# A fused spectral mixer and Mish MLP on one core: w1's first pieces in four transfers, idle matmuls on a built-in constant, the last tile in three column pieces, a new task order

## The chip, the cores and the metric

The kernel runs on one core of one Trainium2 chip. The metric is device time in microseconds, the median over several executions. A profile is one further execution, taken by the hardware profiler. Engines in the profile: PE is TensorE's matmul, PEld its weight load, DVE is VectorE, ACT is ScalarE, POOL is GpSimd, SP is SyncE; ACTq and SPq are the DMA issues of those two.

## The reference, cut to what matters

```python
# x: (1, 2048, 512) bf16
g = sigmoid((x * gate_w).sum(-1, keepdims=True))
a = irfft2(rfft2(x) * (w_r + 1j * w_i), s=(2048, 512))        # spectral branch
h = x @ w1 + b1                                               # w1: 512 x 1792
b = (h * tanh(softplus(h))) @ w2                              # Mish; w2: 1792 x 512
out = g * a + (1 - g) * b
```

## The kernel before, in words

The 2048 rows are 16 tiles of 128 (`NT`), the 1792 hidden columns 14 pieces (`NFT`), the dense branch runs in 4 chunks of 4 tiles (`NCH`). Both branches share TensorE.

Head. SyncE issues the loads of x and most others in a fixed order; ScalarE issues the first pieces of w1 (`ld_w1(0, 4, ...)`, one transfer of 256 rows for each half h of d) and one later piece. GpSimd loads b1 (`braw`). The load of ScalarE's function table (`table`) is a task on ScalarE like any other. Until x is there TensorE runs matmuls whose result nobody reads (`warm0` and on, L425); `NWARM` of them have 256 columns, `NFILL` have 128. They read a tile of zeros that a memset on DVE (L417) makes. Then `tr*` (L476) transpose x, `tr_small` (L484) transposes b1, and `evx*` copy the transposes into `xT`, on DVE or ScalarE.

Dense branch. `mm1_c_ft` (L773) multiplies xT by a piece of w1; `mish_c_ft` (L788) applies Mish on ScalarE into `act`; `mm2_t_0` and `mm2_t_1` (L803) sum the 14 pieces for tile t. In chunk 0 the pieces ft 0 to 3 are cut in four: `mm1a` is tiles 0 and 1, `mm1b` tiles 2 and 3, and the digit behind is the half h of d. For most tiles `bev_t` scales the result out of PSUM (L755 on ScalarE, L756 on DVE) and `sum_t` adds the spectral part; for the last two tiles `fin` (L815) does both in one DVE step. The last tile is computed and stored in two halves of 256 columns.

Spectral branch. `a10`, `a11` (L512) and `s1` (L538) transform forward and go through scratch in DRAM (`r1w`, `r1r`); `s2` (L635) is the second stage; DVE multiplies by the filter (`wm`), GpSimd combines (`wz`), `s2i` (L695) goes back; a second trip through scratch (`r2w`, `r2r`); `s1i` (L723) and `a1i` (L734) finish, with `e5`, `gc`, `sa` and `sb` between and behind.

Order. Each operation is a task with an engine, dependencies and, where it writes PSUM, a bank. The order of every engine, the engine of tasks that can run on either of two, and the banks are not found at build time: they are read from the string `ORDER`, two digits in base 62 for a task, a letter for its engine where there is a choice, a digit for its bank. Each engine runs its tasks strictly in that order. A wait is placed ahead of a task where one of its inputs, or the bank it takes, comes from another engine. `DENSE` and `DENSE2` list the banks that a planner may give to dense products; the digit in `ORDER` decides.

Of the kernel before, what the change touches and what calls it, by code (L numbers as in the profile page):

```python
# [7 lines left out]
BF = mybir.dt.bfloat16  # L8
# [5 lines left out]
NT = 16  # L14
# [151 lines left out]
class _Graph:  # L166
# [89 lines left out]
DIGITS = "0123456789ABCDEFGHIJKLMNOPQRSTUVWXYZabcdefghijklmnopqrstuvwxyz"  # L256
ENGINE = {"p": "pe", "a": "act", "v": "dve", "g": "pool", "s": "sp"}
ORDER = (
    "020L0M0T0500O060N070P03080R090A0Q000B040C010S0D0E0F0U0G0V0H2y0w30W0y70I0J0xv0X0K6k50Y6z11046p00Z11a0a0zv1220b6"
    "u313v1G7701H711Jv6l0c6m721Iv6v736w6x6n6y1K40d7420e1M6o1L10f1461Nv750g1630h15v7670i1Ov1U40j1V27717v1850k1Pv0l1e"  # L260
    "v1W7810m1fv0n7A31Xv0o790p1Yv1A67B0q1C10r1Bv1Za1r70s1Dv1g41i0t19v7C20u2i7E37D20v7G62j7F6q21v1q47H1h26r1s1kv6s7I"
    "16t2k1la7K31jv7J2l7M47L1uv2322m7N2252D67a0241vv1tv1E126v7b25v27v7c37e07d1Fv2C72n7f1Q27g12E2Mv7i01Rv7h331a47j2G"
    "v7k11S1ba2Fv7m02Nv1T7l2Hv1m22o1c7n2O62Y71nv1d7o12Q2a2Z02p7q57p1o2cv1p2P11w32Rv7r7s62Sv1xa7u72dv2bv7t1y2822q7v2"
    "I41z29v7w12Ta2Ja2U62r7x2A7y32Vv2B2e17z2K8002s2fa2L8E62t2W818G72u2X8F2v2g8I58H2h2w8K18J2x8L2z8M2388O0398N3A8Q78"
    "P3B8S68R30318U1328T0v8V347358W4368Y2378X8a08Z3C38b3D63E8c53Mv8e18d3F3Qv3G7O08f3Pv7P3Lv3Sg3H23Y67Qa3I3Ng3Z43a7R"
    "23hv3Rg3b7S3c3mv3Og3d17U07Ta3e3J3iv3K3T7V3lv3jg3U43kg7Wa7X13Wa3Vv3ng3X3u63v23og7Y3w44v3f43v3g8s07Za3p3x48v3q44"
    "5g8t8u13sa3rv46g8w08v47v4G43t8x3y4H68y14Tv4Ag3z28208z4Pv49g834J404I4Qv414K424B9014Uv4Sg4L4922914M84v4N4C44Wg93"
    "8514Da4Ev4O4Vg4F864X4Rg94087a4Y4958814Za4av4b898B08Aa8C4c4d4e8g18Da4f963982979A0999C59B4g34o49D9E04hv4pa4i54w3"
    "9F5444q64xv4j8h55a4l4r4k4t5C04ng5K48ia4s4y55625Dv4mg5La5S38j15Tv4z4vg57514ug505E7595a453g5F5i3585U65ba8k5jv52g"
    "5V5G5Bg5X5H8m05Ag8la5W9av9bv5k59ev5M29c5l8n9dv5N5Ig9f5P5Jg5O8p18oa5Zg5m5n5Rg5c25q49gv5y55d6635Qg5ra5zv9G667a5f"  # L270
    "5pg6055e9H9I75Yg615s39hv8q9J635hg9i5t629jv5v5gg6E68ra5u6M49K764g6Nv6Fa9kv5xg9l6816U3699L5og6Vv6A5wg6B6c365g9Ma"
    "6W56G49N09nv6da9pv6H9mv6X6I6Dg9O9o6Z6Y6Cg6J6ag6O76e39Pa9Q29qv6f6bv9r6P6Lg6g6R9R6Kg6Q6h6Tg9U59sv9S6ig6jv9T9X16S"
    "g9V9W9tv9u9Y9Z"
)
NBF = 14
GD_N = 8
# [5 lines left out]
A1B = (3, 4, 5, 6, 7)  # L282
SPEC = (3, 4, 5, 6, 7)
DENSE = {0: (0, 1, 2, 3), 1: (0, 1), 2: (0, 1), 3: (0, 1)}
DENSE2 = {0: (0, 1), 1: (0, 1), 2: (0, 1), 3: (0, 1)}
NWARM = 12
NFILL = 4
PR = dict(tr=99.0, sp=95.0, mm1=88.0, mish=97.0, mm2=70.0, fin=98.0, gate=96.9, sum=98.5)


def _build(nc, A_x, A_w_r, A_w_i, B_x, B_w1, B_b1, B_w2, gate_w, out):
# [6 lines left out]
    G = _Graph()  # L298
    es = ExitStack()
    with es:  # L300
# [86 lines left out]
        def mm(n):  # L387
            return n / 2400.0 + 0.0025
# [10 lines left out]
        def pe(name, dur, fn, **kw):  # L399
            return G.add(name, "pe", dur, fn, lat=0.17, **kw)  # L400
# [6 lines left out]
        def tt(name, o, i0, i1, op, n, rate=1.0, engs=("dve",), lock=True, **kw):  # L407
# [9 lines left out]
        G.add("wz", "dve", 0.3, lambda e: e.memset(act[:, 2, 0, :], 0.0), writes=["warm"])  # L417
        G.add("ebz", "pool", 0.2, lambda e: e.memset(b1f[:, 0:1], 0.0), writes=["b1z"])
        t_tab = G.add("table", "act", 1.3, lambda e: e.activation(b1f[:, 1:2], b1f[:, 0:1], AF.Mish), reads=["b1z"], writes=["b1t"], prio=0.0)

        pw = _Ps([6])
        tw = []
        for i in range(NWARM + NFILL):
            n = 256 if i < NWARM else 128
            tw.append(pe(f"warm{i}", mm(n), lambda e, n=n: e.matmul(ps[:, pw.bank, 0:n], act[:, 2, 0, 0:128], act[:, 2, 0, 0:n], start=True, stop=True),  # L425
                         reads=["warm"], alloc=pw if i == 0 else None, frees=[pw], prio=0.0, deps=tw[-1:]))
# [5 lines left out]
        def ld_w1(lo, hi, queues):  # L432
            cols = slice(128 * lo, 128 * hi)
            for h in range(2):
                dma(f"ld_w1_{lo}_{h}", w1_sb[:, 2 * h:2 * h + 2, cols], w1v[:, h, :, cols],
                    writes=[("w1", f, h) for f in range(lo, hi)], nbytes=65536 * (hi - lo), bw=340e3, nd=256, queue=queues[h])

# [326 lines left out]
        for c in range(NCH):  # L764
            hb = c % 3
            G.cur_prio = PR["mm1"] - c
            for ft in range(NFT):
                pd = _Ps(DENSE[c])

                def f_mm1(e, c=c, ft=ft, pd=pd, cols=(0, 512), ks=range(4)):  # L770
                    ins = None
                    for i in ks:
                        ins = e.matmul(ps[:, pd.bank, cols[0]:cols[1]], w1_sb[:, i, 128 * ft:128 * (ft + 1)], xT[:, i, 512 * c + cols[0]:512 * c + cols[1]],  # L773
                                       start=(i == 0), stop=(i == 3))
                    return ins

                pr_m = PR["mm1"] - c - 0.06 * ft
                if c == 0 and ft < 4:
                    for part in range(2):
                        for h in range(2):  # L780
                            pe(f"mm1{'ab'[part]}{h}_{ft}", 2 * mm(256), lambda e, f=f_mm1, part=part, h=h: f(e, cols=(256 * part, 256 * part + 256), ks=(2 * h, 2 * h + 1)),
                               reads=[("xT", 2 * part + i, h) for i in range(2)] + [("w1", ft, h)], writes=[("pm", c, ft), ("pmx", ft, part, h)],
                               alloc=pd if part == h == 0 else None, prio=PR["mm1"] + 1.0 - 0.3 * part - 0.06 * h - 0.01 * ft)
                else:
                    pe(f"mm1_{c}_{ft}", 4 * mm(512), f_mm1, reads=[("xT", 4 * c + i, q) for i in range(4) for q in range(2)] + [("w1", ft, 0), ("w1", ft, 1)],
                       writes=[("pm", c, ft)], alloc=pd, deps=mm2s.get(c - 3, ()), prio=pr_m)
                G.add(f"mish_{c}_{ft}", "act", act_dur(512, True),
                      lambda e, ft=ft, pd=pd, hb=hb: e.activation(act[:, hb, ft, :], ps[:, pd.bank, :], AF.Mish, bias=b1f[:, ft:ft + 1]),  # L788
                      reads=[("pm", c, ft), "b1f"], writes=[("act", hb, ft)] + (["warm"] if hb == 2 and ft == 0 else []), frees=[pd], prio=PR["mish"])
            G.cur_prio = PR["mm2"] - c  # L790
            for tl in range(4):
                t = 4 * c + tl

                for part in range(2):
                    if part == 0 or t == NT - 1:
                        pd = _Ps(DENSE2[c])
                    cs_ = slice(256 * part, 256 * part + 256) if t == NT - 1 else slice(0, 512)
                    fts = range(NFT) if t == NT - 1 else range(7 * part, 7 * part + 7)

                    def f_mm2(e, tl=tl, hb=hb, pd=pd, cs_=cs_, fts=fts):  # L800
                        ins = None
                        for ft in fts:
                            ins = e.matmul(ps[:, pd.bank, cs_], act[:, hb, ft, 128 * tl:128 * (tl + 1)], w2_sb[:, ft, cs_],  # L803
                                           start=(ft == 0), stop=(ft == NFT - 1))
                        return ins

                    tk = pe(f"mm2_{t}_{part}", 7 * mm(512), f_mm2,
                       reads=[("act", hb, ft) for ft in range(NFT)] + [("w2", p_) for p_ in ((0, 1) if t == NT - 1 else (part,))],
                       writes=[("pd", t, part if t == NT - 1 else 0)],
                       alloc=pd if part == 0 or t == NT - 1 else None, deps=(mm2s[c][-1:] if t == NT - 1 and part else []))  # L810
# [3 lines left out]
                    G.add(f"fin_{t}_{part}", "dve", dve_dur(256 if t == NT - 1 else 512, True),  # L814
                          lambda e, t=t, pd=pd, cs_=cs_: e.scalar_tensor_tensor(out=xo[:, t, cs_], in0=ps[:, pd.bank, cs_], scalar=omg[:, t:t + 1],  # L815
                                                                                in1=ga[:, t, cs_], op0=ALU.mult, op1=ALU.add),
                          reads=[("pd", t, part if t == NT - 1 else 0), "omg", ("ga", t, "m"), ("ga", t, "p")], writes=[("x", t, part), ("o", t, part)], frees=[pd], prio=PR["fin"])
                    dma(f"out{t}{part}", ov[:, t, cs_], xo[:, t, cs_], reads=[("o", t, part)],
                        nbytes=65536 * (1 if t == NT - 1 else 2), is_out=True, prio=PR["fin"], tail=0.6)
                if t < NBF:  # L820
                    evict_b(t, pd)
        for t in range(NBF):
# [115 lines left out]
```

## Time and profile before

| | us |
|---|---|
| median of 3 runs | 130.19 |
| lowest and highest | 129.87 and 130.69 |
| the profiled execution, its own time | 130.35 |
| its span, first to last instruction | 128.6 |
| TensorE busy | 123.2 |
| DVE, ScalarE, GpSimd busy | 90.9, 70.9, 52.7 |
| HBM read and written | 13.64 MB and 6.29 MB |

The span leaves out 1.75 us of the profiled execution's time, which lie before the first and behind the last instruction. Busy time counts from the first to the last moment of each instruction, and matmuls overlap, so a sum of durations is larger than busy time; in the chain each piece is counted once.

### The profile page before, as it was taken

What the parts mean: (1) busy time and instruction counts of PE and PEld (TensorE: products, weight loads), DVE (VectorE), ACT (ScalarE), POOL (GpSimd) and SP (SyncE); (2) the same over time, 40 slices, a digit from 0 to 9 for tenths busy, and PEclk for the clock granted to TensorE, in tenths of its full rate; (3) what the DMA queues carried; (4) which work ended last, traced back from release to release, by engine and by line L of the source; (5) the groups of instructions that cost most, each with busy time, mean ns of one, the idle gap of its engine ahead of it and who ended that gap; (6) DMA issues with size and microseconds to landing.
All of it is one profiled execution on the core that took longest, in us unless ns stands there. A gap on an engine that the chain in (4) does not pass through costs nothing.

```text
span 128.6 us, 2680 instructions
## 1 busy us (share of the span) xinstructions
PE 123.2 (96%) x1012; PEld 68.0 (53%) x1030; DVE 90.9 (71%) x173; ACT 70.9 (55%) x115; POOL 52.7 (41%) x83
## 2 busy tenths in 40 slices
PE   6999999999999999999999999999999999999992
PEld 4787756645544444444444444444466556555571
DVE  0255999998999711987679994300059999889992
ACT  1347768779898877522228415722597536735400
POOL 4000000001000266079897789200008977895770
PEclk9999999999999999999999999999999999999999
DMA  3999999999945559700040500555930012220313
GB/s 76 341 399 398 281 179 194 169 259 353 342 128 155 171 148 382 290 0 0 5 136 28 163 3 15 158 163 138 392 125 0 5 63 100 84 82 22 147 41 122
DMA packets 18509, 20.11 MB, mean 156 GB/s; under 512 B 1216, under 2 KB 15552, under 8 KB 18368
## 3 DMA queue, kind: packets, MB, share of 16 engines
q1 hardware_dynamic: 17648, 19.15, 49.9%
q10 hardware_dynamic: 816, 0.79, 1.9%
q8 instruction: 8, 0.13, 0.4%
q14 instruction: 5, 0.04, 0.1%
q0 software_dynamic: 32, 0.00, 0.0%
HBM read 13.64 MB, written 6.29 MB: 155 GB/s over the span
## 4 chain that ended last, share of the span: by engine, by line
PE 92%; DMA 3%; ACT 2%; issue 1%; DVE 0%
PE ps L773 38%; PE ps L803 37%; PE ps L476 3%; PE ps L723 3%; PE ps L512 3%; PE ps L734 3%; PE ps L538 3%; DMA xo<-in_A_x_dram 3%; ACT act L788 2%; PE ps L635 1%; ACT xo L755 1%; PE ps L695 0%; DVE xo L815 0%; PE ps L425 0%; PE ps L484 0%
## 5 line engine op out<-in xcount | busy, mean ns | idle before, releaser
L773 PE MATMUL ps<-xT,w_sb 128*128 128x512 bf16 (+1 forms) x231 | 52.5, 367 | 0.6 <-issue 0.2
L803 PE MATMUL ps<-w_sb,act 128*128 128x512 bf16 (+1 forms) x229 | 49.4, 366 | 0.9 <-ACT act L788 0.3
L788 ACT ACTIVATE act<-ps,b1f 128x512 bf16<-128x512 f32 x56 | 38.3, 687 | 17.2 <-PE ps L773 12.5
L803 PEld LDWEIGHTS ps<-w_sb,act 128*128 128x128 bf16 x238 | 22.3, 98 | 22.8 <-issue 0.8
L773 PEld LDWEIGHTS ps<-xT,w_sb 128*128 128x128 bf16 x240 | 22.6, 99 | 21.9 <-issue 0.6
L408 POOL TENSOR_TENSOR Tg<-Qb 128x256 bf16<-128x256 f32 x30 | 22.8, 791 | 20.7 <-DVE Qb L745 20.7
L408 POOL TENSOR_TENSOR Zb<-Qb 128x510 bf16<-128x510 f32 x16 | 20.0, 1268 | 4.7 <-DVE Qb L408 3.8
L755 ACT ACTIVATE xo<-ps,omg 128x512 bf16<-128x512 f32 x13 | 8.9, 687 | 22.9 <-PE ps L803 17.5
L408 DVE TENSOR_TENSOR Qb<-ps,WT 128x1024 f32<-128x1024 f32 x16 | 18.8, 1214 | 0.7 <-POOL Zb L408 0.7
L745 DVE SCALAR_TENSOR_TENSOR Qb<-ps,gcol,Qb 128x256 f32<-128x256 f32 x32 | 13.5, 474 | 0.7 <-POOL Tg L408 0.6
L403 DVE CAST Zb<-ps 128x512 bf16<-128x512 f32 x8 | 5.5, 689 | 11.9 <-PE ps L723 11.8
L403 DVE CAST Ybuf<-ps 128x1024 bf16<-128x1024 f32 x8 | 9.8, 1220 | 5.6 <-PE ps L695 5.1
L408 DVE TENSOR_TENSOR Abuf<-ps,Tg 128x512 bf16<-128x512 f32 x16 | 10.5, 682 | 2.1 <-PE ps L512 2.1
L576 POOL COPY wrv<-WT 128x32 bf16<-128x32 bf16 x2 | 0.4, 227 | 26.6 <-DMA WT<-in_A_w_i_dram 26.6
L554 DVE SCALAR_TENSOR_TENSOR Tg<-xo,Tg 128x512 bf16<-128x512 bf16 x16 | 10.9, 684 | 0.2
L739 ACT ACTIVATE Qb<-ps,gcol 128x256 f32<-128x256 f32 x16 | 7.1, 475 | 4.0 <-PE ps L734 4.0
L408 DVE TENSOR_TENSOR xo<-xo,Tg 128x512 bf16<-128x512 bf16 x14 | 9.1, 678 | 0.0
L403 DVE COPY xT<-ps 128x1024 bf16<-128x1024 bf16 (+1 forms) x9 | 5.2, 595 | 5.3 <-PE ps L476 5.3
L559 POOL TENSOR_TENSOR gcol<-omg,gdot 128x16 f32<-128x16 f32 x1 | 2.9, 2942 | 14.5 <-DVE Tg L554 14.5
L404 ACT ACTIVATE Ybuf<-ps 128x1024 bf16<-128x1024 f32 x8 | 8.2, 1021 | 0.1
L734 PE MATMUL ps<-GMs,Zb 128*128 128x128 bf16 x64 | 5.5, 219 | 0.0
L476 PE MATMUL ps<-ident,xo 128*128 128x128 bf16 x64 | 5.4, 236 | 0.1
(61 smaller groups left out, 84.2 us busy)
## 6 DMA issues: line engine op xcount, KB each, us to landing
Abuf<-scr SPq DMA_DIRECT2D x8, 512.0 KB, 5.6
scr<-Ybuf SPq DMA_DIRECT2D x16, 128.0 KB, 2.2
scr<-Ybuf SPq DMA_DIRECT2D x4, 512.0 KB, 2.9
w_sb<-in_B_w_dram SPq DMA_DIRECT2D x2, 896.0 KB, 12.7
out_dram<-xo SPq DMA_DIRECT2D x7, 256.0 KB, 2.0
xo<-in_A_x_dram SPq DMA_DIRECT2D x3, 512.0 KB, 7.6
rt<-c_rt SPq DMA_DIRECT2D x2, 512.0 KB, 8.8
WT<-in_A_w_r_dram SPq DMA_DIRECT2D x7, 128.5 KB, 11.0
```

The source lines that it names most:

```text
L403: fs = {"dve": ("dve", dve_dur(n, rate=rate), lambda e: e.tensor_copy(out=dst(), in_=src())), "act": ("act", act_dur(n), lambda e: e.activ ...
L404: "act": ("act", act_dur(n), lambda e: e.activation(dst(), src(), AF.Copy))}
L408: f = lambda e: e.tensor_tensor(out=o(), in0=i0(), in1=i1(), op=op)
L476: ins = e.transpose(psb[:, pt.bank, o:o + 128], xo[:, t0 + i, d0:d0 + 255:2], ident[:, :])
L554: lambda e, t=t: e.scalar_tensor_tensor(out=junk, in0=xo[:, t, :], scalar=1.0, in1=gwb, op0=ALU.mult, op1=ALU.mult, accum_out=gdot[:, t:t ...
L734: ins = e.matmul(ps[:, p5.bank, 128 * i:128 * i + 128], TT[:, sl, 2 * par + ri, :], GMs[:, i, :], start=True, stop=True)
L739: lambda e, t=t, sl=sl, p5=p5: e.activation(gC[:, sl, :].rearrange("p (i n) -> p i n", i=2), ps[:, p5.bank, :].rearrange("p (i n) -> p i n ...
L745: lambda e, t=t, sl=sl, p5=p5, o=o, op=op: e.scalar_tensor_tensor(out=st1[:, sl, o::2, :], in0=ps[:, p5.bank, :].rearrange("p (i n) -> p i ...
L755: G.add_multi(f"bev_{t}", [("act", act_dur(512, True), lambda e: e.activation(xo[:, t, :], ps[:, pd.bank, :], AF.Copy, scale=omg[:, t:t + ...
L773: ins = e.matmul(ps[:, pd.bank, cols[0]:cols[1]], w1_sb[:, i, 128 * ft:128 * (ft + 1)], xT[:, i, 512 * c + cols[0]:512 * c + cols[1]], sta ...
L788: lambda e, ft=ft, pd=pd, hb=hb: e.activation(act[:, hb, ft, :], ps[:, pd.bank, :], AF.Mish, bias=b1f[:, ft:ft + 1]),
L803: ins = e.matmul(ps[:, pd.bank, cs_], act[:, hb, ft, 128 * tl:128 * (tl + 1)], w2_sb[:, ft, cs_], start=(ft == 0), stop=(ft == NFT - 1))
```

## The change

Four things are edited.

- The first pieces of w1 (`lo == 0`) are loaded by quarters of d: four transfers of 128 rows on ScalarE's queue instead of two of 256. Both quarters of a half have to be there before a product reads them; the new key `w1a` says so.
- The idle matmuls read a constant 1.0 that the language's start-up code has in SBUF anyway, and the memset task `wz` is gone. There are 16 of 256 columns and 2 of 128; before there were 12 and 4.
- The last tile comes in three column pieces, `LAST`: 256, 128 and 128 columns, each with its own 14 products, `fin` and store.
- `ORDER` is new. Read as lists: all 18 idle matmuls come before the first transpose (before, 13 did, and three followed); the 16 first transposes and `tr_small` come before the first dense product; on ScalarE `table` stands right behind the first of the four w1 transfers, ahead of the other three; `evx0a` and `evx0b` move from DVE to ScalarE, `evx2a` the other way; `e1f_8`, `e1f_10`, `e4_00`, `e4_10` and `bev_4` move from DVE to ScalarE, `bev_8` and `bev_13` to DVE; in the middle the spectral tasks come earlier and the dense products of chunk 3 later. `DENSE2` lets the planner give more banks to chunks 2 and 3.

```diff
 ORDER = (
...
-DENSE2 = {0: (0, 1), 1: (0, 1), 2: (0, 1), 3: (0, 1)}
-NWARM = 12
-NFILL = 4
+DENSE2 = {0: (0, 1), 1: (0, 1), 2: (0, 1, 2, 7), 3: (0, 1, 2, 7)}
+LAST = ((0, 256), (256, 384), (384, 512))
+NWARM = 16
+NFILL = 2
...
-        G.add("wz", "dve", 0.3, lambda e: e.memset(act[:, 2, 0, :], 0.0), writes=["warm"])
...
-            tw.append(pe(f"warm{i}", mm(n), lambda e, n=n: e.matmul(ps[:, pw.bank, 0:n], act[:, 2, 0, 0:128], act[:, 2, 0, 0:n], start=True, stop=True),
-                         reads=["warm"], alloc=pw if i == 0 else None, frees=[pw], prio=0.0, deps=tw[-1:]))
+            tw.append(pe(f"warm{i}", mm(n), lambda e, n=n: e.matmul(ps[:, pw.bank, 0:n], nc.const_aps.tensor(1.0, [128, 128], BF), nc.const_aps.tensor(1.0, [128, n], BF), start=True, stop=True),
+                         alloc=pw if i == 0 else None, frees=[pw], prio=0.0, deps=tw[-1:]))
...
             for h in range(2):
+                for i in range(2) if lo == 0 else ():
+                    dma(f"ld_w1_{lo}_{h}{'ab'[i]}", w1_sb[:, 2 * h + i, cols], w1v[:, h, i, cols],
+                        writes=[(("w1a", "w1")[i], f, h) for f in range(lo, hi)], nbytes=32768 * (hi - lo), bw=340e3, nd=128, queue=queues[h], issue=0.45)
+                if lo == 0:
+                    continue
...
-                for part in range(2):
+                for part in range(len(LAST) if t == NT - 1 else 2):
                     if part == 0 or t == NT - 1:
                         pd = _Ps(DENSE2[c])
-                    cs_ = slice(256 * part, 256 * part + 256) if t == NT - 1 else slice(0, 512)
+                    cs_ = slice(*LAST[part]) if t == NT - 1 else slice(0, 512)
```

The remaining lines of the diff follow from these: the products of chunk 0 read `w1a` too, `mish` no longer owns the tile of zeros, and the sizes of `fin` and of the last stores are taken from the piece.

More of the change, by code (lines that the diff above doesn't have):

```diff
@@ L258 @@
 ORDER = (
[L259 to L273, printed above, removed]
+    "020M0N0400W05030R0607080S090A0T0B0O0C0D0P0V0E0F0Q0X0G0H0U0Y0I310J000K0L0Z010z40a1170b10a13614v1550c1J46x216v6n"
@@ new lines @@
+    "00d12a7211K0e1Mv6y0f6z73741Lv0g756o6p760h1N3701P1O47710i711Qv0j6q1Rv7817319618v6r1Av7970k1iv0l1X07A7B21Sv0m1hv"
+    "1Z0n1Y77D10o1av0p1k01bv0q7E0r7C0s0t1ca1B50u1D41Cv1F30v1Ev1j60w1T11l1Gv7F70x1Uv1u41t57G7H323v1v1V7J61mv7I1W1xv7"
+    "L27K24v6s11wv7M7N51yv2l7P37O1nv1H72m7Q6t2541Iv1oa2F6277d02n2H7f32Qv7e2Pv1d57g2G02671ea2Jv7h228v362Ka7j37i1f29v"
+    "1p41g2Iv7k2R62S21qv2Aa6u2T6v7l06w2Vv1r1z67m2Uv2B31s20a7n12o2Cv2b22Wa2c07o212L52d222p2Ma2D7p72ev7r12E2q7q7t42N2"
+    "fv7s2O2r2X67u7v02gv2Yv2h47w7x12s2Z2ia2t3772a7z27y2j2u810802k2v831822w8H4842x3B8J38I2y3C8L2388K3D2z8N63E8M300y8"
@@ new lines @@
+    "P78O328Q7R0393334353A7S3F47Ta3G23Ov7U13I3Pv7V3Tv3Qg7X07Wa3H3Sv3J3Rg3b63c43d3K33kv3Ug7Y3L3e3Vg3ov8R17Za8T23lv3f"
+    "8S3M3N3g37a03W8U3h3pv3ng8V73mg8X18W3rg3X28Y3x63Za7b3i47v3qg3Ya3z46v8Z13j7ca3a3s3y28a3t449g4Av8b03ua48g4Bv8513v"
+    "a408c4Cg3w4J24K44Tv8d0414Dg427864M8e434Sv44454L4E8804Xv4Ug87a4Wv4N8f14Vg4O6898g4Zg4P4F38Aa4Yg8h14Ga4Hv4Q8v08i4"
+    "R4I4a8x28w4b38y8z14cv4da912904e8B692933950944f8C964g4h8E54i8Da8F8j78Ga4j64r04z44ka5734sv8k58a50v4t34l58lv5164u"
+    "5F44m5N04v5975Ga8m14w5Oa4o4yg524n5A4xg8n54534pg5C5B55g5P65H58oa5V49hv8p35Q5Eg5Wa5S5I4qg5R5d48q5Dg5J5K56g5ev5Mg"
@@ L274 @@
+    "8s08ra9jv9kv5l49gv9l5t35Lg5ma5X25uv8t9i5Y5Tg5Z5Ug5a6149718ua9mv9nv62a5f35cg9909o985g5bg5v69B19A5i9pv5w6305h9D4"
+    "9C5y5kg5x645n79F59E5jg65665o60g9H49G5q5zg5p9J19I9qv6925sg9r6H79K6Av9L05rg6Ia6B69tv6P19M6J59sv6X76C6Qv6f367g9N2"
+    "9u6K6D6ga68g6E6L6Gg9O6Yv6Fg6M9vv6R69wv9Q09Pa6Og6S9x6Ng6U6Z46T9R6a9yv6Wg6b6c6Vg9T69Sv6ev9zv6h09U6dvA06i6j6k9X39"
+    "V6mg9W6lv9a19Y9d49Z9b9c9e9f"
 )
@@ L781, in _build @@
                             pe(f"mm1{'ab'[part]}{h}_{ft}", 2 * mm(256), lambda e, f=f_mm1, part=part, h=h: f(e, cols=(256 * part, 256 * part + 256), ks=(2 * h, 2 * h + 1)),
-                               reads=[("xT", 2 * part + i, h) for i in range(2)] + [("w1", ft, h)], writes=[("pm", c, ft), ("pmx", ft, part, h)],
+                               reads=[("xT", 2 * part + i, h) for i in range(2)] + [("w1", ft, h), ("w1a", ft, h)], writes=[("pm", c, ft), ("pmx", ft, part, h)],
                                alloc=pd if part == h == 0 else None, prio=PR["mm1"] + 1.0 - 0.3 * part - 0.06 * h - 0.01 * ft)
                 else:
-                    pe(f"mm1_{c}_{ft}", 4 * mm(512), f_mm1, reads=[("xT", 4 * c + i, q) for i in range(4) for q in range(2)] + [("w1", ft, 0), ("w1", ft, 1)],
+                    pe(f"mm1_{c}_{ft}", 4 * mm(512), f_mm1, reads=[("xT", 4 * c + i, q) for i in range(4) for q in range(2)] + [(k, ft, h) for h in range(2) for k in ("w1", "w1a")],
                        writes=[("pm", c, ft)], alloc=pd, deps=mm2s.get(c - 3, ()), prio=pr_m)
@@ L788, in _build @@
                       lambda e, ft=ft, pd=pd, hb=hb: e.activation(act[:, hb, ft, :], ps[:, pd.bank, :], AF.Mish, bias=b1f[:, ft:ft + 1]),
-                      reads=[("pm", c, ft), "b1f"], writes=[("act", hb, ft)] + (["warm"] if hb == 2 and ft == 0 else []), frees=[pd], prio=PR["mish"])
+                      reads=[("pm", c, ft), "b1f"], writes=[("act", hb, ft)], frees=[pd], prio=PR["mish"])
             G.cur_prio = PR["mm2"] - c
@@ L805, in f_mm2 @@
                         return ins
-                    tk = pe(f"mm2_{t}_{part}", 7 * mm(512), f_mm2,
+                    tk = pe(f"mm2_{t}_{part}", 14 * mm(cs_.stop - cs_.start) if t == NT - 1 else 7 * mm(512), f_mm2,
                        reads=[("act", hb, ft) for ft in range(NFT)] + [("w2", p_) for p_ in ((0, 1) if t == NT - 1 else (part,))],
@@ L813, in _build @@
                         continue
-                    G.add(f"fin_{t}_{part}", "dve", dve_dur(256 if t == NT - 1 else 512, True),
+                    G.add(f"fin_{t}_{part}", "dve", dve_dur(cs_.stop - cs_.start, True),
                           lambda e, t=t, pd=pd, cs_=cs_: e.scalar_tensor_tensor(out=xo[:, t, cs_], in0=ps[:, pd.bank, cs_], scalar=omg[:, t:t + 1],
@@ L818, in _build @@
                     dma(f"out{t}{part}", ov[:, t, cs_], xo[:, t, cs_], reads=[("o", t, part)],
-                        nbytes=65536 * (1 if t == NT - 1 else 2), is_out=True, prio=PR["fin"], tail=0.6)
+                        nbytes=256 * (cs_.stop - cs_.start), is_out=True, prio=PR["fin"], tail=0.6)
                 if t < NBF:
```

## The prediction

> **What bounds the kernel now.** I read the page first, then the waits, then the chain of waits from the head on, then the order of each engine as the two order strings spell it.
>
> ```profile
> span 128.6 us, 2680 instructions
> PE 123.2 (96%) x1012; PEld 68.0 (53%) x1030; DVE 90.9 (71%) x173; ACT 70.9 (55%) x115; POOL 52.7 (41%) x83
> PEclk9999999999999999999999999999999999999999
> PE 92%; DMA 3%; ACT 2%; issue 1%; DVE 0%
> ```
>
> TensorE is busy 96% of the span and makes 92% of the chain of work. No change of order can save more than what is not useful product: the head, small losses between, the tail. Head (timeline, then the chain: start, length, what):
>
> ```profile
> 0.80 0.87 SPq L373 DMA_DIRECT2D xo<-in_A_x_dram  x2
> 0.80 1.95 ACTq L373 DMA_DIRECT2D w_sb<-in_B_w_dram  x3
> 0.92 0.27 DVE L417 MEMSET act<- 128x256 uint32 x1 [0.92 <-PEq L923]
> 1.25 2.85 PE L425 MATMUL ps<-act 128*128 128x256 bf16 x13 [1.25 <-DVE act L417]
> 1.30 0.79 POOL L373 DMA_DIRECT2D braw<-in_B_b_dram  x1 [0.80 <-POOLq L923]
> 2.78 1.28 ACT L419 ACT_TABLE_LOAD   x1 [2.78 <-issue]
> 4.08 0.20 ACT L419 ACTIVATE b1f<-b1f 128x1 f32<-128x1 f32 x1
> ...
> 0.80 3.35 DMA xo<-in_A_x_dram
> 4.19 1.03 PE ps L476 x8
> 5.22 0.32 PE ps L425 x3
> 5.54 0.85 PE ps L773 x4
> 6.40 0.43 PE ps L476 x4
> 6.82 0.28 PE ps L773 x2
> 7.11 0.22 PE ps L476 x4
> 7.33 0.22 PE ps L773 x2
> 7.55 0.11 PE ps L484
> 11.04 0.89 PE ps L476 x16
> ```
>
> Useful work starts at 4.19, when x has landed (0.80 + 3.35). Until about 6.85 the array runs at half rate, though the clock row shows nothing of it: four products of 256 columns take 0.85 (0.213 each), four transposes 0.43 (0.107 each). From 7.11 on the same take 0.108 and 0.055. By 7.66 (7.55 + 0.11) it has done 16 transposes, the small one of b1 and 8 products of 256 columns. Summing the steps ahead of a point on TensorE from such rows, tr4 (11.04) has 5.08 us of full-rate work ahead of it.
>
> **The change part by part.** *Idle matmuls.* The memset on DVE goes (0.27), and with it TensorE's wait. The memset itself began at 0.92, released by the opening barrier, so I let TensorE start at 0.92 instead of 1.25. Now 16 of 256 columns at 0.213 and 2 of 128 at 0.107 come ahead of all transposes: 3.63 us, to 4.55. That is 0.36 later than the 4.19 of before. In exchange the three fillers (0.32) between the transposes are gone, and so is the 0.17 by which the first eight transposes exceed 8 x 0.107.
>
> If the array goes to full rate at the same moment, 6.85: 16 transposes take 1.71, to 6.26; the small one 0.11, to 6.37; until 6.85 there are 2.25 products at half rate, and the remaining 5.75 take 0.62, to 7.47. Before it was 7.66: **0.19 won**. What this path waits for:
>
> ```profile
> xo<-in_A_x_dram SPq DMA_DIRECT2D x2, 256.0 KB, 3.8
> w_sb<-in_B_w_dram ACTq DMA_DIRECT2D x3, 256.0 KB, 5.6
> braw<-in_B_b_dram POOLq DMA_DIRECT2D x1, 3.5 KB, 4.4
> 1.00:2.00 1.00, 0.75 (x4) 0.57 (x5) 0.19 (x1) 0.00 (x0) 0.70 (x1) 1.00 0.15 27
> 4.00:7.10 3.10, 3.01 (x25) 2.56 (x25) 0.85 (x2) 0.50 (x3) 0.00 (x0) 1.00 1.02 344
> 6.86 0.60 ACT L404 ACTIVATE xT<-ps 128x512 bf16<-128x512 bf16 x1 [2.58 <-PE ps L476]
> ```
>
> The second piece of x landed 4.3 after its issue (the median of two is their mean, the first took 3.35), at about 5.5; the third pair of transposes now comes at 5.41, so it costs 0.1 at most, and x should come sooner, since less of w1 is in its way. The row of b1 landed at 5.70 and starts one small memset later; it is wanted at 6.26.
>
> *w1 by quarters.* Four issues of 128 rows (0.44 each, as the x rows: 0.87 for two) replace two of 0.65. But in the new order the table load stands behind the first one. ScalarE: 0.80 + 0.44 + 1.28 + 0.20 = 2.72, then quarters at 2.72, 3.16 and 3.60, then the third old transfer, free at 4.7. Queued behind are the first two copies of transposes, moved here from DVE; they are ready at about 5.2 and 5.6, so ScalarE is in time, and its 0.60 a copy (to 5.8 and 6.4) ends before TensorE wants them (6.37 and 7.25). A quarter lands no useful product early, because the first product reads both quarters of its half. When does the last come? Data begin near the end of the second microsecond (27 GB/s in it, 0.80 issue), so about 1.1 after an issue: here from 3.82. From 4 on DMA moves 344 GB/s; half of it for the ScalarE queue, 172, brings 384 KB by 6.1. Before, its first 512 KB were there at 1.45 + 5.6 = 7.05, 100 GB/s with the slow start in it; at that rate 7.7. I take 150, past the start: 6.4 (an estimate from these rows). The first product of the second half comes after six others, at 7.25. So **0**, with 0.85 to spare; at 7.7 it costs 0.45, and if a quarter needs the old 5.6 from its own issue, the last lands at 9.2 and it costs 1.95.
>
> *The order between.* Both lists hold the same useful TensorE work, 119.2 us. What moves is when: the first spectral product of stage 2 has 42.2 us ahead of it instead of 45.2, the last back product 70.9 instead of 75.2, the last stage starts after 82.5 instead of 86.8. The data must come as much sooner.
>
> ```profile
> 45.05 1.77 SPq L373 DMA_DIRECT2D Abuf<-scr  x4
> 51.24 0.56 PE ps L635 x32
> 79.83 1.26 POOL L408 TENSOR_TENSOR Zb<-Qb 128x510 bf16<-128x510 f32 x1
> 81.90 0.64 PE L695 MATMUL ps<-Zb,rt 32*64 32x256 bf16 x32
> DMA to landing us min/median/max: 4.3/4.3/4.3
> L408 DVE TENSOR_TENSOR Qb<-ps,WT 128x1024 f32<-128x1024 f32 x16 | 18.8, 1214 | 0.7 <-POOL Zb L408 0.7
> L403 DVE CAST Ybuf<-ps 128x1024 bf16<-128x1024 f32 x8 | 9.8, 1220 | 5.6 <-PE ps L695 5.1
> L408 POOL TENSOR_TENSOR Zb<-Qb 128x510 bf16<-128x510 f32 x16 | 20.0, 1268 | 4.7 <-DVE Qb L408 3.8
> 120.06 6.04 PE ps L803 x41
> ```
>
> Stage 1 to 2: the first read back from scratch was issued at 45.05 and landed 4.3 later (the row of that one issue), at 49.35; TensorE used it at 51.24, 1.9 spare. In the new list the last product of stage 1, which that read waits for, has 30.9 ahead of it, not 33.5, so the data move up 2.6 and the use 3.0: 1.5 spare. Stage 2: TensorE's work from its first to its last group shrinks from 30.0 to 28.7 us. There POOL's sixteen products (20.0) and DVE's (18.8) set the pace: POOL ended at 81.09, the last back product began at 81.90. The new order takes two evictions of 1.22 and a scaled one of 512 columns (0.74, as the row of that size in the tail below) off DVE here, and POOL starts after two DVE products of 1.21 instead of three; that pays for the 1.3. By the lists the back products then stand 0.5 to 1 us behind POOL's results, as before. Stage 2 to 3: 11.6 us of other work cover the second trip through scratch, the same in both lists. So **0** in the middle. Bounds: tr4 lies 5.96 behind its sum, the last 41 products (120.06, 113.1 ahead) 6.94, so at best 1.0 can be won; at worst the 1.3 of stage 2 is lost.
>
> *Last tile in three.*
>
> ```profile
> 126.13 0.48 DVE xo L815
> 123.27 0.74 DVE L815 SCALAR_TENSOR_TENSOR xo<-ps,omg,Tg 128x512 bf16<-128x512 f32 x1
> out_dram<-xo SPq DMA_DIRECT2D x2, 64.0 KB, 1.6
> out_dram<-xo SPq DMA_DIRECT2D x1, 128.0 KB, 1.7
> ```
>
> 28 products of 128 columns at 0.056 replace 14 of 256 at 0.108: +0.05. The last DVE step shrinks from 0.48 by half of what 256 columns more cost (0.74 - 0.48): -0.13. The last store carries 32 KB, not 64: 0.1 for 64 KB less between the two rows gives -0.05 (bounds: -0.1 and +0.1). The extra store is issued in the 0.78 between two pieces. Sum **-0.13**.
>
> [...]
>
> **Sum.** The profiled execution took 130.35 in all, 1.75 beside its span of 128.6. 130.35 - 0.19 + 0 + 0 - 0.13 = 130.03; it lay 0.16 over the median of the three runs (130.19), so **129.9** by the median.
>
> **The rivals.** *Early clock (faster).* The idle matmuls now run 3.63 without a gap, where before 2.85 did, and half rate might end during them. If it ends at 3.48, TensorE is through them at 4.0 and waits for x (4.14), then its second piece (5.2 to 5.5), b1 (5.8) and the second half of w1 (6.4): 8 products done at about 6.87, 0.79 before 7.66. Time 130.19 - 0.79 - 0.13 = 129.3, or 128.3 with the 1.0 of the middle. For it: the unbroken run; against it: before, the rate rose only 5.6 after the first idle matmul. [...]
>
> *Late quarters (slower).* The three quarters behind the table load need the old 5.6 each: stall of 1.95 at the first product of the second half, 129.9 + 1.95 = 131.8. It decides from a landing after 7.25. For it: TensorE has all its later work behind that product; against it: the old 5.6 was mostly queueing, and fewer bytes stand ahead of the quarters.
>
> *Stage 2 too tight (slower).* POOL's last product ends as long after the first stage-2 group as before (29.9) and TensorE, 1.3 sooner, waits: 131.2. For it: DVE's 5 buffers tie it to POOL; against it: the 3.2 us taken off DVE.
>
> *The change does nothing:* quarters unused, order neutral, head a wash: 130.1, inside the forecast.
>
> **How the numbers follow.** A measurement of this kernel tells about 1% (1.3 us) from no change. Forecast, with doing nothing: 0.48; early clock 0.22; late quarters 0.12; stage 2 0.18. Faster by over 1% (under 128.9) needs the early clock with part of the middle, half of 0.22, and 0.06 of the forecast's edge: 0.17. Slower (over 131.5): 0.11 of the late quarters, 0.15 of stage 2 with a wait elsewhere added: 0.26. Same: 0.57. The forecast's own range is 129.3 to 130.6; to leave out no more than 2 in 10 it reaches 128.7 and 131.9.
>
> **What would show it.** Right: no memset on DVE at 0.92, idle matmuls from about 0.9 to 4.5 with no gap, transposes at half rate from then, full rate near 6.9, the first stage-2 group near 48.1, the last back product near 77 without a wait, DVE's last step 0.35 long. Wrong: transposes at 0.055 from the start (early clock); a DMA wait of TensorE near 7.2 (late quarters); a wait on POOL in stage 2; TensorE's end not within 0.5 us of 125.8.

## The result and the profile after

The changed kernel takes 130.82 us (median of 6, 130.53 to 131.1), the kernel before 130.19 in the same session: ratio 1.0072, 95% interval 1.0047 to 1.0097. It is 0.6 us slower, where 0.3 faster was forecast. The profiled execution took 130.92, 0.57 more than the profiled one of before.

The page of the changed kernel, its first line and the shares of the chain by engine:

```profile
span 129.2 us, 2736 instructions
...
PE 87%; DMA 9%; ACTq 1%; ACT 0%; issue 0%; DVE 0%; SPq 0%
```

TensorE's share of the chain fell from 92% to 87% and DMA's rose from 3% to 9%. So the question is which transfers are in it. The waits of TensorE (the page's columns: us in total, times, longest), and the chain around the two DMAs (start, length, what):

```profile
PE ps L425 <- PEq L928: 0.8, 1, 0.8
PE ps L778 <- DMA w_sb<-in_B_w_dram: 0.8, 1, 0.8
PE ps L728 <- DMA Abuf<-scr: 0.2, 1, 0.2
```

```profile
2.20 0.45 ACTq L374
...
2.69 7.15 DMA w_sb<-in_B_w_dram
...
9.97 1.24 PE ps L778 x6
11.21 0.89 PE ps L481 x16
...
85.26 4.63 DMA Abuf<-scr
...
89.94 1.07 PE ps L728 x16
...
126.94 0.35 DVE xo L820
```

The new wait of 0.8 is not for a quarter. It is for a transfer that the change doesn't edit: the later piece of w1 (columns of ft 4 to 7, second half, 256 rows of 1 KB), which stands behind the quarters on ScalarE's queue. It is issued at 2.69, lands 7.15 later at 9.84, and `mm1_0_4`, which reads it, starts at 9.97. The head on TensorE, ScalarE and their queues (timeline: start, us, engine, line):

```profile
0.83 3.79 PE L425 MATMUL ps<-const-bfloat16-1.0 128*128 128x256 bf16 x18 [0.83 <-PEq L928]
4.41 1.74 PE L481 MATMUL ps<-ident,xo 128*128 128x128 bf16 x16
...
6.20 2.36 PE L778 MATMUL ps<-xT,w_sb 128*128 128x256 bf16 x20
8.83 0.39 PE L517 MATMUL ps<-FMs,Tg 128*128 128x128 bf16 x4
9.97 0.81 PE L778 MATMUL ps<-xT,w_sb 128*128 128x512 bf16 x3 [0.76 <-DMA w_sb<-in_B_w_dram]
1.23 1.28 ACT L419 ACT_TABLE_LOAD   x1 [1.23 <-PEq L928]
1.30 1.36 ACTq L374 DMA_DIRECT2D w_sb<-in_B_w_dram  x3
2.69 0.63 ACTq L374 DMA_DIRECT2D w_sb<-in_B_w_dram  x1
5.53 0.45 PEld L481 LDWEIGHTS ps<-ident,xo 128*128 128x128 bf16 x8 [0.32 <-DMA xo<-in_A_x_dram]
```

The first 20 products of ft 0 to 3 run from 6.20 without a wait, those of the second half among them, so every quarter was there in time: the last one was issued at 2.20 and landed 4.4 later, at 6.60, and the first product of the second half, the seventh of the 20, came at about 6.85. The last four products that TensorE may run before `mm1_0_4` (`a11_0`, of the spectral branch) start at 8.83 and follow each other at 0.055; by 9.05 the next could start, and TensorE stands until 9.97, 0.9 us. (The page's 0.8 counts from the modelled end of the last of the four, 8.83 + 0.39.)

The sum by the prediction's own yardstick (a start, less the full-rate work ahead of it): tr4 starts at 11.21 with 4.87 ahead, so 6.34 behind; before it was 5.96. Without the wait of 0.9 it would be 5.44: the head won 0.52. From there to the end of TensorE another 1.37 is lost (before 0.98, so +0.39), the third piece of the last tile adds 0.05 of products, and the tail is 0.2 shorter. -0.52 + 0.90 + 0.39 + 0.05 - 0.2 = 0.6, the difference of the two spans (129.2 and 128.6).

### The profile page after: what moved, and what is told of

It reads as the page before. It is cut to its first block, busy times and chain, and to the rows that moved or that the text cites. A ratio compares the mean times of both kernels' runs of the same rounds, so it can differ in the third digit from the quotient of the medians.

```text
span 129.2 us, 2736 instructions
## 1 busy us (share of the span) xinstructions
PE 125.1 (97%) x1046; PEld 68.2 (53%) x1046; DVE 88.6 (69%) x169; ACT 73.2 (57%) x120; POOL 51.9 (40%) x82
## 4 chain that ended last, share of the span: by engine, by line
PE 87%; DMA 9%; ACTq 1%; ACT 0%; issue 0%; DVE 0%; SPq 0%
PE ps L778 36%; PE ps L808 34%; DMA w_sb<-in_B_w_dram 6%; DMA Abuf<-scr 4%; PE ps L728 3%; PE ps L739 3%; PE ps L543 3%; PE ps L517 2%; PE ps L481 2%; PE ps L640 2%; PE ps L700 2%; ACTq L374 1%; ACT L419 0%; DVE xo L820 0%; PE ps L657 0%
## 5 line engine op out<-in xcount | busy, mean ns | idle before, releaser
L778 PE MATMUL ps<-xT,w_sb 128*128 128x512 bf16 (+1 forms) x240 | 53.5, 365 | 0.8 <-DMA w_sb<-in_B_w_dram 0.8
L808 PE MATMUL ps<-w_sb,act 128*128 128x512 bf16 (+2 forms) x252 | 51.5, 355 | 0.0
L409 POOL TENSOR_TENSOR Tg<-Qb 128x256 bf16<-128x256 f32 x29 | 22.0, 785 | 25.9 <-DVE Qb L750 25.8
L760 ACT ACTIVATE xo<-ps,omg 128x512 bf16<-128x512 f32 x12 | 8.2, 687 | 20.1 <-PE ps L808 20.1
L404 DVE CAST Zb<-ps 128x512 bf16<-128x512 f32 x7 | 4.7, 683 | 11.4 <-PE ps L728 11.4
L405 ACT ACTIVATE Ybuf<-ps 128x1024 bf16<-128x1024 f32 x10 | 10.0, 1020 | 0.3 <-PE ps L700 0.3
L404 DVE CAST Ybuf<-ps 128x1024 bf16<-128x1024 f32 x6 | 7.3, 1221 | 4.0 <-PE ps L700 4.0
L404 DVE COPY xT<-ps 128x1024 bf16<-128x1024 bf16 (+1 forms) x8 | 4.6, 620 | 7.1 <-PE ps L481 7.1
L405 ACT ACTIVATE Zb<-ps 128x512 bf16<-128x512 f32 x9 | 5.3, 597 | 2.5 <-PE ps L728 2.5
L739 PEld LDWEIGHTS ps<-GMs,Zb 128*128 128x128 bf16 x64 | 4.5, 98 | 2.4 <-DVE Zb L404 0.2
## 6 DMA issues: line engine op xcount, KB each, us to landing
scr<-Ybuf SPq DMA_DIRECT2D x16, 128.0 KB, 3.9
```

What stands on the lines that cost most here:

```text
L404: fs = {"dve": ("dve", dve_dur(n, rate=rate), lambda e: e.tensor_copy(out=dst(), in_=src())), "act": ("act", act_dur(n), lambda e: e.activ ...
L405: "act": ("act", act_dur(n), lambda e: e.activation(dst(), src(), AF.Copy))}
L409: f = lambda e: e.tensor_tensor(out=o(), in0=i0(), in1=i1(), op=op)
L739: ins = e.matmul(ps[:, p5.bank, 128 * i:128 * i + 128], TT[:, sl, 2 * par + ri, :], GMs[:, i, :], start=True, stop=True)
L760: G.add_multi(f"bev_{t}", [("act", act_dur(512, True), lambda e: e.activation(xo[:, t, :], ps[:, pd.bank, :], AF.Copy, scale=omg[:, t:t + ...
```

## The experiments

Theory after the result: the quarters cost about 0.9 us, not by landing late but by what is queued behind them; the rest of the change wins a little. Rivals: the new order or the idle matmuls cost it, or the four transfers as such. Ratios are to the kernel before on the same chip in the same session, with 95% intervals; its median was 129.87 or 130.16 there, so times of different runs are compared by their ratios. Wherever an edit changes a list of tasks, `ORDER` is encoded anew with the rest of the order as it was.

**Undo the quarters (a_halves).** The changed kernel with `ld_w1` as before:

```diff
-                for i in range(2) if lo == 0 else ():
-                    dma(f"ld_w1_{lo}_{h}{'ab'[i]}", w1_sb[:, 2 * h + i, cols], w1v[:, h, i, cols], ...
-                if lo == 0:
-                    continue
```

> The changed kernel with the old two transfers of 256 rows for the first pieces of w1; all else, the new order too, is kept. Theory of the late piece: in the changed kernel the third transfer of ScalarE's queue (columns 4 to 7 of w1, second half) is issued at 2.69 instead of 2.06 and lands at 9.84, while TensorE could use it at 9.05; with two transfers its issue goes back to about 2.1 and its landing to 8.5 or 8.7, the wait of 0.9 goes, and the time falls from 130.8 to about 129.9. Rival, the order alone: the new order reads that piece about 1 us sooner than the old one did (old: 10.0), so a wait stays even with two transfers, half of it or more, and the time stays above 130.4.

129.75 us (12 runs), ratio 0.9985 (0.9966 to 1.0005), where the changed kernel had 1.0072: 1.07 us less by the two medians, which come from two sessions. One session holds such a pair, both with other idle matmuls (a_idle512 and a_halves_idle512, below): 130.92 and 129.81, 1.11 apart. The wait for w1 is gone; what is left in the head, besides the start, is the second piece of x:

```profile
PE ps L476 <- DMA xo<-in_A_x_dram: 0.2, 1, 0.2
```

In that kernel the later piece is the second of two issues that take 1.2 from 1.5 on, so it is issued at about 2.1; it landed 5.8 later, at about 7.9. The DMA queues in windows (packets, MB, share of 16 engines; q1 is SyncE's, q10 ScalarE's), first the changed kernel from 7.4 to 8.2 and from 8.2 to 9.0:

```profile
q1 hardware_dynamic: 68, 0.25, 78.8%
q10 hardware_dynamic: 65, 0.06, 22.0%
...
q1 hardware_dynamic: 84, 0.29, 92.0%
q10 hardware_dynamic: 37, 0.03, 12.6%
```

then the kernel with two transfers, from 7.4 to 8.2:

```profile
q1 hardware_dynamic: 112, 0.33, 106.3%
q10 hardware_dynamic: 2, 0.00, 0.4%
```

From 7.4 to 8.2 in the changed kernel about as many packets of the one queue pass as of the other (65 and 68), but those of q10 carry about 1 KB (0.06 MB over 65) and those of q1 3.7 KB: the later rows of x, 4 KB each. So q10 had 22.0% of the time there, and 12.6% from 8.2 to 9.0, with 37 packets against 84; and 0.6 us of a later issue became 1.9 of a later landing (7.9 to 9.84).

**The quarters alone (b_quarters).** The kernel before with that edit only, in the old order:

> The kernel before, order and all, with the quarters alone. Late-piece theory: the later piece is issued at about 2.6 instead of 2.06 and lands at 9.2 to 9.9 instead of 8.5, but the old order reads it only at 10.0, so no wait: time within 0.3 us of the kernel before. Rival, the quarters are slow whatever the order: 0.5 us or more slower.

130.75 us (7 runs), ratio 1.0082 (1.0051 to 1.0113). I had the old order reach the piece too late to wait for it; that was a miss. The chain shows the same transfer, issued at the same time:

```profile
2.70 7.35 DMA w_sb<-in_B_w_dram
...
10.40 0.81 PE ps L778 x3
```

So the quarters carry the whole loss by themselves in the old order too (+0.88 by the medians). The two profiled executions differ by less, 0.39, and at this very place: `mm1_0_4` started at 10.40 here and at 10.01 before. How long TensorE waits for the piece depends on how early it gets there: in b_last3 (below), which has the head of before, full rate came earlier and `mm1_0_4` started at 9.21.

**Quarters kept, the piece moved (a_piece_sp).** The changed kernel with the later piece on SyncE's queue, ahead of the later rows of x:

```diff
-        ld_w1(4, 8, ("sp", "act"))
+        ld_w1(4, 8, ("sp", "sp"))
```

> The changed kernel with its four quarters, but the later piece of w1 (columns 4 to 7, second half) issued on SyncE's queue behind its first half, ahead of the x rows of 4 KB. Theory of the late piece, sharpened: on ScalarE's queue its 1 KB packets took turns one for one with x's 4 KB packets from 7.4 on and had 22% and then 13% of the DMA time; ahead of x on the same queue it has no such rival and lands at 8.2 to 8.8 at the latest, the wait of 0.9 goes, time 129.7 to 130.0, as with two transfers. Rival, the quarters cost by themselves (four issues, more packets): a wait of over 0.4 stays somewhere in the head, time over 130.3. The fourth to seventh tiles of x land some 0.5 later; a small wait for them is possible in both.

129.90 us (12 runs), ratio 1.0001 (0.9978 to 1.0024). The quarters are all there, the wait is not: the only wait left on TensorE up to 14 us is the one for the start.

```profile
PE ps L425 <- PEq L928: 0.8, 1, 0.8
```

That falsifies the rival that four transfers cost by their number, and with the two runs above settles the cause: the piece queued behind them, late on that queue. (One packet for one held from 7.4 to 8.2 alone: 65 and 68 there, 37 and 84 from 8.2 to 9.0.)

**The piece late, without quarters (a_halves_piece).** Two transfers, but the later piece waits for the table load:

```diff
-... nd=256, queue=queues[h])
+... nd=256, queue=queues[h], deps=[t_tab] if lo == 4 and h else ())
```

> The kernel after with w1's first pieces in two transfers of 256 rows again, and one thing more: the later piece of w1 (columns of tiles 4 to 7, second half) waits on ScalarE until the table load and the small activation behind it are done. It is so issued at about 2.95, where the kernel after issues it at 2.69 and the kernel with two transfers at 2.1; the table load and the number of transfers are those of the latter. If the late issue of this piece is the whole price of the quarters, it lands at 9.5 to 10.3, TensorE waits 0.6 to 1.3 for it at the fifth product group, and the time is 130.4 to 131.0 (ratio 1.005 to 1.009). Rival: the four transfers themselves (their number, the room they take on the queue) are the price; then the piece still lands before 9 and the time stays at 129.75 (ratio 0.9985).

The edit overshot: in the list used here both first transfers stand ahead of the table load, so the piece was issued at 3.63 and not at 2.95.

```profile
3.63 8.13 DMA w_sb<-in_B_w_dram
...
12.28 1.92 PE ps L773 x5
PE ps L773 <- DMA w_sb<-in_B_w_dram: 3.0, 1, 3.0
PEclk9997799999999999999999999999999999999999
```

The wait is 3.0, so two transfers with a late piece bring back what four had cost. (0.5 of it lies between the landing at 11.76 and the start at 12.28; what took that is open.) The doses stand in line: issued at 2.1 no wait, at 2.69 one of 0.9, at 3.63 one of 3.0; between the last two, 0.94 of issue cost 1.92 of landing (9.84 to 11.76) and 2.1 of waiting. The time is 133.74 (131.72 to 133.9, 6 runs), which isn't the price of the wait alone: in five of the six executions the granted clock fell besides (mean 0.987; the two digits 7 of the row). The five products recorded in that row, of 512 and 256 columns, take 1.92 in the chain, where the same place takes 1.03 in the kernel with two transfers. The one execution with a clock of 1.000 took 131.72, 1.6 over the median of the kernel before in that session (130.16); a single execution gives no firm size. In the changed kernel, behind its gap of 0.9, the granted clock was 1.00 (from 10 to 48).

**The idle matmuls in other sizes.** Eight of 512 columns instead of 16 of 256, in the changed kernel (a_idle512) and without quarters (a_halves_idle512); 32 of 128 without quarters (a_halves_idle128). The edit of the first two:

```diff
-NWARM = 16
+NWARM = 8
-            n = 256 if i < NWARM else 128
+            n = 512 if i < NWARM else 128
```

> The changed kernel with its 16 idle matmuls of 256 columns made 8 of 512: the same idle time, 8 matmuls and 8 weight loads fewer in TensorE's stream. Theory of the instruction fetch: in the changed kernel the last store to the second scratch took 5.1 us to land instead of 2.9, because a 16 KB fetch of TensorE's instructions sat for 1.85 us on one of its DMA engines (81.05 to 82.90); 16 instructions fewer move that fetch about 1.7 us later, behind the store's data; the store lands in 2.9, TensorE's wait at the start of the last stage (0.2 to 0.35) goes, time about 130.5. Rival, a store that is slow for another reason (bank, chance): it stays at about 5 and the time at 130.8. The wait for w1 stays in both.

> Both of the two edits: two transfers for the first pieces of w1, and 8 idle matmuls of 512 columns. If the two waits are separate, their gains add: 129.5 to 129.6, under the kernel before by 0.6. If the second wait only fills the room that the first one leaves (or the reverse), it equals the better of the two single edits.

> The changed kernel with two transfers for w1 and its 16 idle matmuls of 256 columns made 32 of 128: the same idle time, 32 TensorE instructions more. Theory of the instruction fetch: the 16 KB fetches move against the work; if the one near the last store to the second scratch no longer lies within the 2 us of its data, the store lands in 2.9 instead of 4.7. Eight matmuls fewer moved that fetch by only 0.6 and left it on the store (5.1). Time as with 16, about 129.8, since that store is not waited for once w1 is in time. Rival, no link between fetch and store: a store of 4 to 5 us without a fetch beside it, or one of 2.9 with a fetch on it.

In this order: 130.92, ratio 1.0071 (1.0043 to 1.0100); 129.81, 0.9997 (0.9980 to 1.0015); 130.03, 1.0014 (0.9995 to 1.0034). The size makes no difference that these runs can tell. The first is the most telling: its profiled execution had full rate from about 4.0 (transposes in the window from 4.0 to 5.0, mean of one):

```profile
L481 PE MATMUL ps<-ident,xo 128*128 128x128 bf16 x6 | 0.5, 221 | 0.4 <-DMA xo<-in_A_x_dram 0.4
...
2.70 7.76 DMA w_sb<-in_B_w_dram
```

(the same take 314 at half rate, below), and still it is no faster: it only comes sooner to the same transfer, which here lands at 10.46 (2.70 + 7.76). An earlier clock was worth nothing as long as that piece came late.

The theory of the instruction fetch missed its time in the first (the fetch moved too little and stayed on the store, which took 5.1 again) but gave the store's time in the third. There the store, issued at 79.4, landed in 2.9; in the same kernel with 16 of 256 columns (a_halves) the fetch began at 80.75 to 81.0, behind the issue at 79.2, and the store took 4.7. The two kernels of the comparison divide in the same way: 5.1 in the changed one, where the fetch began at 81.05, 1.1 behind the issue at 79.95, and 2.9 in the one before, where it began at 83.0, ahead of the issue at 83.9. The same store took 4.3 in a_halves_idle512 and 2.9 in b_quarters. It is not in the time, since without quarters TensorE doesn't wait for that store.

**A tile of zeros instead of the constant (a_halves_zero).** Without quarters, with `wz` and the wait for it put back:

> The changed kernel with two transfers for w1, and the idle matmuls back on the tile of zeros that DVE fills first. Theory of the early start: in the changed kernel the idle matmuls began at 0.83 instead of 1.25 and ran without a gap, and full rate began at about 5.5 instead of 6.9; with the tile of zeros they begin at 1.25, end 0.4 later, full rate comes later (6 to 7), and TensorE reaches the first full product 0.4 to 0.8 later than with the constant, all of it in the time: 130.3 to 130.7 if the wait for w1 is gone. Rival: the waits behind the head (second piece of x, w1) take it up, and it costs less than 0.2 against the same kernel with the constant.

130.07 us (12 runs), ratio 1.0009 (0.9983 to 1.0035), 0.3 over the constant (129.75); the intervals overlap, and 0.3 lies between the theory (0.4 to 0.8) and its rival (under 0.2), so this run decides nothing.

**The constant alone (b_const15).** The kernel before with 15 of 256 and 4 of 128 columns on the constant:

> The kernel before with the idle matmuls alone changed: they read the built-in constant instead of a tile that VectorE sets to zero, and 15 of 256 and 4 of 128 columns stand there, all but the three fillers of before ahead of the transposes. The old order, the old two transfers and the old last tile stay. Theory: they start at 0.83 instead of 1.25 and full rate comes earlier, near 5.3 instead of 6.9; TensorE is then bounded by the second piece of x and b1, and 0.2 to 0.5 is won: 129.4 to 129.7 (ratio 0.996 to 0.9985). Rival: the later pieces of w1 and x bound the head anyway and nothing comes of it: 129.87 (ratio 1.000), with a DMA wait of TensorE between 5 and 11 that grows by what the clock gave.

130.25 us (12 runs, 129.56 to 130.69), ratio 1.0001 (0.9975 to 1.0027): a miss. The idle matmuls did start at 0.83, but in the profiled execution full rate came no sooner. Products and transposes in the window from 5.1 to 6.0 (count, busy, mean ns of one), this kernel first and then the changed one from 5.3 to 6.1:

```profile
L772 PE MATMUL ps<-xT,w_sb 128*128 128x256 bf16 x4 | 1.1, 421 | 0.0
L475 PE MATMUL ps<-ident,xo 128*128 128x128 bf16 x1 | 0.3, 314 | 0.0
```

```profile
L481 PE MATMUL ps<-ident,xo 128*128 128x128 bf16 x10 | 1.0, 239 | 0.1
```

The mean of one is 314 at half rate and 220 at full rate; 239 is a mixture, so the changed kernel turned over in this window.

**The last tile.** Three pieces in the old order (b_last3), and two pieces in the new order without quarters (a_halves_two). The edit of the second; the first puts the line with three pieces into the kernel before:

```diff
-LAST = ((0, 256), (256, 384), (384, 512))
+LAST = ((0, 256), (256, 512))
```

> The kernel before with the last tile in three pieces alone. By the two profiles the last DVE step took 0.35 instead of 0.48 and the last store 1.4 instead of 1.6, for 0.05 more of TensorE: 0.2 to 0.3 us faster, ratio 0.998. Rival: rows of 256 bytes or the extra issue eat it up, no difference or slower.

> The kernel after with two transfers of 256 rows, and with the last tile in two pieces of 256 columns again, as in the kernel before; the new order otherwise. Theory: the three pieces win in this order what the prediction said, so this kernel is 0.13 to 0.25 slower than the one with three pieces (129.75): 129.9 to 130.0 (ratio 1.000), with a last step of VectorE of 0.48 and a last store of 64 KB of about 1.6. Rival: nothing comes of three pieces here either, as in the old order, and it stays at 129.75 (ratio 0.9985).

129.99, ratio 1.0019 (0.9998 to 1.0041), and 130.12, ratio 0.9988 (0.9964 to 1.0012), against 0.9985 with three pieces. Neither tells three pieces from two by its time. The rows of the tail do, in the new order; with three pieces, then with two (timeline and DMA issues):

```profile
125.85 0.35 DVE L815 SCALAR_TENSOR_TENSOR xo<-ps,omg,Tg 128x128 bf16<-128x128 f32 x1 [0.43 <-PE ps L803]
out_dram<-xo SPq DMA_DIRECT2D x2, 32.0 KB, 1.4
```

```profile
125.58 0.48 DVE L815 SCALAR_TENSOR_TENSOR xo<-ps,omg,Tg 128x256 bf16<-128x256 f32 x1 [1.05 <-PE ps L803]
out_dram<-xo SPq DMA_DIRECT2D x2, 64.0 KB, 1.5
```

From the start of that step to the end of the span (128.1 and 128.0) it is 2.25 with three pieces and 2.42 with two: 0.2, which fits the forecast's 0.13 and is too small for the time. In the old order nothing was won there: with three pieces it is 2.64 (125.36 to 128.0), and the stores of 32 KB took 1.7; with two, in the kernel before, it is 2.47 (126.13 to 128.6).

**More room for x (a_x_first).** Without quarters, and with w1's second half and its later pieces behind the second x rows on SyncE's queue:

```diff
-        ld_w1(0, 4, ("act", "act"))
+        ld_w1(0, 4, ("act", "sp"))
-        ld_w1(4, 8, ("sp", "act"))
+        ld_w1(4, 8, ("sp", "sp"))
```

> The kernel after with two transfers of 256 rows, and the loads on the queues dealt out so that x has more room at the start: ScalarE's queue carries only the first half of w1's first pieces, and SyncE's queue carries the first x rows, the second x rows, then the second half of w1's first pieces and the later pieces. The small transpose of b1 stands behind the first products. Theory: the second x rows land at 4.9 to 5.2 instead of 5.5 to 5.65, the first product comes near 5.9 instead of 6.4, and where full rate is early 0.3 to 0.4 is won: 129.4 (ratio 0.996). Rival: the w1 half behind x, or the later pieces, take it back: TensorE waits for a DMA between 6.5 and 10, and the time is 129.75 or more (ratio 0.9985 and up).

129.87 us (12 runs), ratio 0.9989 (0.9961 to 1.0017). The first product did come sooner, at 5.91 (6.46 in the kernel with two transfers), though the second piece of x came only 0.2 sooner (the transposes that read it began at 5.45 against 5.68); the rest is an earlier full rate in that execution and the transpose of b1, which stands behind. Nothing came of it: in the profiled execution, the slowest of the 12 at 131.33, the last-issued rows of x, behind ten other issues on the one queue, came late:

```profile
6.66 10.18 DMA xo<-in_A_x_dram
...
16.89 0.62 PE ps L476 x8
```

That wait was 1.3. It is the rival's story with another transfer: what is moved ahead on a queue makes something else last. No version here is faster than the kernel before by more than these runs can tell.

## Why the prediction was wrong

The step that failed is "*w1 by quarters*", with its **0** "with 0.85 to spare". Of the quarters themselves it was right that they cost nothing: the last landed at 6.60 (6.4 forecast), the first product of the second half had them in time, and 1.95 was not paid. The margin was 0.25, since that product came at about 6.85 and not at 7.25. But the step ended the queue with "then the third old transfer, free at 4.7" and did not ask who reads that third transfer and when. Its reader is `mm1_0_4`, which TensorE was free to start at 9.05; it landed at 9.84 instead of about 7.9, and the step's true value was +0.9 in the profiled execution (by the medians +0.88 alone in b_quarters, +1.07 by a_halves). The rival "Late quarters" had the right queue and the wrong transfer: 131.8 and a stall near 7.2, where it was 130.8 and 9.05.

The half of the DMA bandwidth that the step gave to ScalarE's queue was about right while the quarters landed (44.9% of the engines' time from 4 to 5, 62.0% from 5 to 6), but not behind them: beside the rows of 4 KB it was 22.0% and 12.6%.

The same step was wrong in a second place. It put the issues behind the table load at 2.72, 3.16 and 3.60. The load ran from 1.23 to 2.51, and ScalarE's queue issued three transfers from 1.30 on, under it. Had it blocked them, the piece would have been issued near 4 instead of 2.69; by a_halves_piece (3.63, wait 3.0) that would cost over 3 us, an estimate. So this error hid nothing: it made the case look worse, and the reader was still not asked for.

*Idle matmuls*: -0.19 forecast, -0.52 in the profiled execution before the wait. They started at 0.83, not 0.92, ended at 4.41, not 4.55, and full rate came between 5.3 and 6.1, not at 6.85. The rival "Early clock" was so half right: at full rate TensorE waited for the second piece of x, as it said. Whether the idle matmuls did that stays open. Other executions with near the same head had full rate late (b_const15, after 6.0) or early (b_last3, with the old head: transposes at 219 from 5.1), and b_const15's median is that of before. That half rate ends at 3.48, and that an unbroken run of idle matmuls ends it, was the author's assumption, and no run shows it: full rate came from about 4.0 in a_idle512, between 5.3 and 6.1 in the changed kernel, and after 6.0 in b_const15, whose idle matmuls ran from 0.83 to 4.30.

*The order between*: 0 forecast. From tr4 to the end of TensorE the kernel with two transfers loses 0.99 and the kernel before 0.98, so 0 was right for the order itself. In the changed kernel the first stage-2 group started at 48.53 and the last back product at 78.06, and no matmul waited for GpSimd, so "Stage 2 too tight" fell. What the changed kernel loses more, 0.39, goes with the second trip through scratch. Its last store there took 5.1, against 2.9 before, and the read that it releases (85.26) was waited for by 0.2, counted from the modelled end of the product ahead. By the starts it is the whole: the first product behind the read starts 1.08 later than in the kernel with two transfers (89.94 and 88.86), where tr4 started 0.71 later (11.21 and 10.50). Store and fetch:

```profile
q8 instruction: 1, 0.02, 1.8%
scr<-Ybuf SPq DMA_DIRECT2D x1, 512.0 KB, 5.1
```

The trace shows a fetch of instructions (16 KB, the q8 row of the window from 79.5 to 86; 1.8% of 16 engines there is 1.9 us of one) beside the store. Without quarters the store is late as well (4.7), but the fetch and the store fall otherwise against TensorE, and nobody waits. In a_halves_idle128, where only the idle matmuls were cut differently, the store landed in 2.9. That agrees with a fetch that delays it; no run proves it.

*Last tile*: -0.13 forecast, 0.2 by the rows. The stores with rows of 256 bytes landed in 1.4 (1.7 in b_last3), the two of 64 KB before in 1.6.

Take the failed step out and the time comes near the forecast's 129.9: 129.75 without quarters, 129.90 with the piece moved. In part that is luck. In those sessions the kernel before itself took 129.87, and by their ratios (0.9985 and 1.0001) neither version differs from it; the 0.3 that was forecast as won is not shown. In the profiled executions the kernel with two transfers is 0.54 under the one of before (129.81 and 130.35), 0.33 of it ahead of tr4 and 0.2 in the tail, but the head's part goes with the moment of full rate, which varies from one execution to the next.

## What to carry to other kernels

When a transfer is cut in pieces, follow the queue to its last entry, not to the last piece: the entry behind was issued 0.6 us later here (2.69 and 2.1), and its reader was the one to look for. It has rows of 1 KB and came into the time of a transfer with rows of 4 KB on another queue, and the 0.6 us became 1.9 at its landing. And once a wait for data ends a stage, a faster engine ahead of it is worth nothing there (a_idle512: full rate from about 4.0, the time 130.92).

## What the runs showed of the hardware that was not expected

- From 7.4 to 8.2 in the changed kernel the two queues passed 65 and 68 packets, of about 1 KB and 3.7 KB, in 22.0% and 78.8% of the DMA engines' time; from 8.2 to 9.0 it was 37 and 84 packets, 12.6% and 92.0%.
- Issues on ScalarE's queue went on under a table load (three from 1.30 on, the load from 1.23 to 2.51).
- The wait of 3.0 in a_halves_piece was not the whole loss: behind it the granted clock was 0.67 from 12.2 to 16.0, and the profiled execution took 133.82, 2.1 over the one execution of that kernel whose clock stayed at 1.000.
- The last 512 KB store to scratch took 2.9 in the kernel before, where a 16 KB fetch of instructions began 0.9 ahead of its issue, and 5.1 and 4.7 in the changed kernel and a_halves, where the fetch began 1.1 and 1.5 to 1.8 behind it.
- With the same head, full rate came near 5.0 in one execution (b_last3) and near 6.9 in another (before), so a single profile doesn't tell what idle matmuls are worth.
